# Row E in column tiles of TensorE, and another order of loads at the start of a fused Fourier and gated feed-forward kernel

## The chip, the cores and the metric

The kernel runs on one core of one Trainium2 chip. The metric is the device time of one execution in microseconds (us), as the median of several runs; lower is better. The engines are TensorE (PE, with its weight loads as PEld), VectorE (DVE), ScalarE (ACT), GpSimd (POOL) and SyncE (SP, which here only issues transfers). They run side by side, each through its own instructions in order, and wait for each other by semaphores.

## What is computed

The reference, cut to what matters:

```python
x: (8, 3008, 256) float32
X = fft(fft(x, axis=1), axis=2).real        # (8, 3008, 256)
t = X.reshape(24064, 256)
gate = 1 / (1 + exp(-(t @ w_gate)))         # w_gate, w_val: (256, 1536)
val = t @ w_val
return (gate * val) @ w_out                 # w_out: (1536, 256)
```

The three weight matrices arrive as float64.

## The kernel before

**The sequence transform.** For each of the eight batches the transform along the 3008 points is a matrix product with cosine and sine tables `st`. The symmetries of the transform leave 1505 of the 3008 rows and a quarter of the points: `fold_ops` adds and subtracts the mirrored parts of `x` (tile `x4`), first along the points, then along the features, on VectorE and GpSimd. Six matmuls of 126 x 377 or 126 x 376 (`half`, even and odd points in banks `ev` and `od`) give one half of a result; one ScalarE copy and two VectorE operations (`places`) spread it over the even or odd columns of one of three tiles of 1505 columns each: `pk` (cosine part), `qk` (sine part) and `ek`. The last, `ek`, is the row E: the transform of the single feature in the middle (feature 128), the same in all 128 partitions.

**Where E comes from.** For batch 0, before, `ek` is computed as `pk` is: the weights of the matmul are feature 128 broadcast to 128 columns, so that all partitions come out equal. For batches 1 to 7 the rows are made at once in the loop (`e_load`, `e_fold`, `e_rows`, `e_out`): a matmul with 7 columns of weights, one for each batch, the rows `er` stored to memory (`ed`), and one row spread over 128 partitions by a transfer when its batch begins (`seq_start`).

**The weights.** The feature transform is merged into the weights: `merge` multiplies a piece of `w_gate` or `w_val` (256 columns) with the table `dt` into `G1` and `G2`, four matmuls into a bank `ps`, two ScalarE copies, and two transfers that turn one row of `G2` into columns `ge`. A piece of `w_out` is brought into seven forms `wf` on ScalarE and GpSimd (`forms`). Before either, a piece must become float32: `weight_load` fetches 512 KB as pairs of integers, `weight_parts` is two ScalarE operations, `weight_join` three VectorE operations and one of GpSimd. There are 18 pieces, in the order of `jobs`.

**The loop.** Its unit is a step `i`: one block of 128 hidden features for 256 columns. `front` makes two products `pa` and `pb` on TensorE, and VectorE computes `ae` (two operations, `ek` times the column `ge` plus `pa`) and two tiles `z`; ScalarE applies the sigmoid; `gate` is the product `h` on VectorE in the step after, and sums `sf` on GpSimd; `back`, four steps behind, multiplies with `wf` into the banks `po`. Twelve steps fill one block of output columns, and `finish` stores it. Banks for `pa`, `pb`, `ps`, `ev` and `od` come from one pool of four. Work beside the steps is listed by hand: `at(i, f)` puts `f` into step i, `pre` puts it ahead of the sigmoid.

**Order at the start.** Nothing reorders instructions: what is written first on an engine runs first. Transfers of SyncE and ScalarE use eight semaphores in turn, so that a transfer may have to wait for the eighth before it. Before, two pieces are loaded first, then `x` of batch 0, the cosine table in two halves, four pieces, the sine table whole, and four more pieces. Pieces 0 and 1 are converted and merged; then batch 0 is folded in two halves of the points, with cosine and E sums after each; the sine sums follow; the conversion of pieces 2 to 8 is placed between the evacuations of the sums. The step after which the loop starts holds the merge of piece 2 alone; pieces 9 to 17 are converted in steps 0 to 8, and merges stand in steps 0 to 8.

Of the kernel before, what the change touches and what calls it, by code (L numbers as in the profile page):

```python
# [45 lines left out]
def kernel(  # L46
# [45 lines left out]
    def mm(o, l, r, start, stop):  # L92
        nc.tensor.matmul(o, l, r, start=start, stop=stop, skip_group_check=True)  # L93
# [19 lines left out]
    ge = const.tile([P, 2, NFT], F32, name="ge")  # L113

    x8 = const.tile([NP, B - 1, 4, NQ], F32, name="x8")
    ed = dram.tile([B - 1, NK], F32, name="ed")

    def load_table(t, nq):
        for q in range(0, NQ, nq):
            nc.sync.dma_start(out=st[:, t, q : q + nq], in_=stab[:, t, q : q + nq])  # L120

    jobs = [(w, c - (w == 2)) for c in range(NPR + 1) for w in range(3)
            if (c if w == 2 else c < NPR)]
    RAW, WS = {}, {}
    shared = {}
    KEEP = 10

    def weight_load(j):  # L130


        w, c = jobs[j]
        src = (moe_w_gate, moe_w_val, moe_w_out)[w]
        src = src[2 * c * P : 2 * (c + 1) * P, :] if w == 2 else src[:, c * WC : (c + 1) * WC]
        src = src.rearrange("(c p) f -> p c f", p=P)

        def some(n, pool, tag):

            key = tag, (j - 6) // 3 if tag == "c7" else 0  # L140
            if key not in shared:
                shared[key] = pool.tile([P, n, 2 * WC], F32, name=f"w{tag}", tag=tag)
            return shared[key]

        if j < KEEP:
            pool, tag = ((zp, "z"), (pqp, ("pk", "qk", "ek")[j % 3]), (op, "os"), (sp, "sf"))[
                j // 3 if j < 6 else j // 2 - 1]
            raw = pool.tile([P, 2, WC, 2], I32, name="raw", tag=tag)
            if j < 6:
                pool, tag = ((app, "ae"), (hp, "h"))[j // 3]  # L150
                ws = pool.tile([P, 2, WC], F32, name="ws", tag=tag)
            else:
                ws = some(3, cp, "c7")[:, (j - 6) % 3].rearrange("p (c f) -> p c f", c=2)
        else:
            both = some(12, xp, "x4")
            r, i = (j - KEEP) % 3 * 2, 6 + (j - KEEP) % 6
            raw = both[:, r : r + 2].rearrange("p a n -> p (a n)").bitcast(I32).rearrange(
                "p (c f w) -> p c f w", c=2, w=2)
            ws = both[:, i].rearrange("p (c f) -> p c f", c=2)
        WS[j] = ws  # L160
        if src.dtype == F32:
            nc.sync.dma_start(out=ws, in_=src)
        else:
            RAW[j] = raw
            nc.sync.dma_start(out=raw.rearrange("p c f w -> p c (f w)"), in_=src.bitcast(I32))

    def weight_parts(j):

        if j in RAW:
            raw, ws = RAW[j], WS[j]  # L170
            lo, hi = raw[:, :, :, 0], raw[:, :, :, 1]
            nc.scalar.activation(ws, hi.bitcast(F32), AF.Abs)
            nc.scalar.activation(lo, lo.bitcast(U32), AF.Copy, scale=2.0 ** -29)

    def weight_join(j):
        if j not in RAW:
            return
        raw, ws = RAW.pop(j), WS[j]
        lo, hi = raw[:, :, :, 0], raw[:, :, :, 1]
        wi = ws.bitcast(I32)  # L180
        ts = nc.vector.tensor_scalar
        ts(out=ws, in0=ws, scalar1=2.0 ** -15, scalar2=HUGE, op0=ALU.max, op1=ALU.min)
        ts(out=wi, in0=wi, scalar1=3, scalar2=0x3FFFFFF8, op0=ALU.logical_shift_left,
           op1=ALU.bitwise_and)
        nc.vector.scalar_tensor_tensor(out=wi, in0=hi, scalar=-(2 ** 30), in1=wi,
                                       op0=ALU.bitwise_and, op1=ALU.bitwise_or)
        nc.gpsimd.tensor_tensor(wi, wi, lo, op=ALU.add)
# [36 lines left out]
    def fold_ops(b, nq):  # L224
# [60 lines left out]
    def half(w, d, blk, sn, rows, other=None):  # L285


        c0, n = ((0, NE), (NE, NO))[blk]
        ev, od = [bank(name, other and other[i])[0:rows, 0:n] for i, name in enumerate(("ev", "od"))]

        def sums(*qs):
            for q in sorted(qs, key=lambda q: q % 2):
                mm((ev, od)[q % 2], w(q), st[:, int(sn), q, c0 : c0 + n], q < 2, q >= NQ - 2)

        def then():
            a = evp.tile([P, NE], F32, name="a", tag="a")[0:rows, 0:n]
            nc.scalar.copy(a, ev)
            return lambda: places(a)

        def places(a):  # L300
            nc.vector.tensor_tensor(d[:, blk : blk + 2 * n - 1 : 2], a, od, op=ALU.add)
            lo, hi = (od, a) if sn else (a, od)
            top = M - blk
            nc.vector.tensor_tensor(d[:, top : top - 2 * NO + 1 : -2], lo[:, 0:NO], hi[:, 0:NO],
                                    op=ALU.subtract)
        return sums, then

    def whole(sums, then):
        sums(*range(NQ))
        return then()  # L310

    def seq_start(b):
        PQE[b] = (pqp.tile([P, NK], F32, name="pk", tag="pk"),
                  pqp.tile([P, NK], F32, name="qk", tag="qk"),
                  pqp.tile([P, NK], F32, name="ek", tag="ek"))
        if b:
            nc.sync.dma_start(out=PQE[b][2], in_=ed[b - 1 : b, :].to_broadcast([P, NK]))

    def seq_group(b, blk, what, other=None):
        return half(lambda q: W[b, blk][what][:, q, :], PQE[b][what], blk, what == 1, P, other)  # L320


    ER = []

    def e_load():
        for b in range(1, B):
# [18 lines left out]
    chunks = [(k0, min(CH, NK - k0)) for k0 in range(0, NK, CH)]  # L345
# [147 lines left out]

    def weight_round(*js):
        for j in js:
            weight_parts(j)
            weight_join(j)
# [24 lines left out]

    per = 2 * NPR * len(chunks)
    side = {}
# [111 lines left out]
```

## Time and profile before

| | us |
|---|---|
| time, median of 3 runs | 2027.57 |
| lowest and highest | 2027.19, 2031.57 |
| span of the profiled execution | 2028.5 |

```profile
## 2 busy tenths in 40 slices
PE   5999999999999999999999999999999999999998
PEld 3788789888998889888898888988889888898888
DVE  6899778987899878997889977999879988898887
ACT  3422222222222222222222222222222222222222
POOL 3679555875569755696457955589446875565655
```

Each digit is the busy share of a fortieth of the span (some 51 us) in tenths. Only the first slice shows TensorE half idle: it is the start, with the loads and the first batch's transform. The second holds the early steps, in which the conversion of the weights is done beside the loop. From there on TensorE is full.

### The profile page before, as it was taken

The page shows a single profiled execution, that of the slowest core. Times are in us where ns is not written, and L with a number is a line of the kernel's source. Part 1 is how long each engine was busy: PE and PEld are TensorE (multiplying, and loading weights), DVE is VectorE, ACT ScalarE, POOL GpSimd, SP SyncE. Part 2 cuts the span into 40 slices and gives each one's busy share as a digit, 9 for nine tenths or more (in the row PEclk, how much of TensorE's full clock was granted, in tenths as well). Part 3 has the DMA queues.
Part 4 walks back from the last instruction along what each step waited for, and adds up shares of the span by engine and source line. Part 5 has one row for each costly group of instructions (what it writes and reads, how often), then busy time and mean ns, then how long its engine had stood idle before and what let it go on. Part 6 is the DMA issues. An engine that isn't in the chain of part 4 may idle for free.

```text
span 2028.5 us, 27347 instructions
## 1 busy us (share of the span) xinstructions
PE 1996.6 (98%) x9168; PEld 1743.3 (86%) x9168; DVE 1754.9 (87%) x3221; ACT 498.5 (25%) x875; POOL 1328.4 (65%) x1675
## 2 busy tenths in 40 slices
PE   5999999999999999999999999999999999999998
PEld 3788789888998889888898888988889888898888
DVE  6899778987899878997889977999879988898887
ACT  3422222222222222222222222222222222222222
POOL 3679555875569755696457955589446875565655
PEclk8999999999999999999999999999999999999999
DMA  8240002100021000200010000201002010000001
GB/s 260 84 74 11 27 11 74 33 12 11 11 81 27 11 11 17 76 26 11 16 60 28 27 16 16 73 10 37 11 11 72 16 31 11 11 16 16 11 16 26
DMA packets 136176, 70.98 MB, mean 35 GB/s; under 512 B 127875, under 2 KB 128131, under 8 KB 133642
## 3 DMA queue, kind: packets, MB, share of 16 engines
q1 hardware_dynamic: 134214, 68.69, 12.6%
q8 instruction: 74, 1.21, 0.3%
q10 hardware_dynamic: 1822, 0.54, 0.1%
q14 instruction: 66, 0.54, 0.1%
HBM read 44.50 MB, written 24.68 MB: 34 GB/s over the span
## 4 chain that ended last, share of the span: by engine, by line
PE 85%; DVE 7%; POOL 4%; DMA 2%; issue 1%; ACT 0%; DVEq 0%; SPq 0%; ACTq 0%; POOLq 0%
PE po L93 37%; PE pa L93 21%; PE pb L93 21%; PE ev L93 3%; PE od L93 3%; DVE ae L364 2%; DVE h L379 2%; DVE z L368 1%; DMA ge<-G 1%; DVE z L367 1%; POOL x L239 1%; POOL x L237 1%; DMA st<-in_stab_dram 1%; POOL sf L384 1%; POOL sf L383 1%
## 5 line engine op out<-in xcount | busy, mean ns | idle before, releaser
L575 ACT ACTIVATE z<-z 128x512 f32<-128x512 f32 (+1 forms) x576 | 358.5, 622 | 1319.1 <-DVE z L368 1319.1
L364 DVE SCALAR_TENSOR_TENSOR ae<-ek,ge,pa 128x256 f32<-128x256 f32 (+1 forms) x1152 | 489.7, 466 | 186.1 <-PE pa L93 181.9
L93 PE MATMUL pb<-qk,G 128*128 128x256 f32 (+1 forms) x2304 | 582.2, 375 | 2.5 <-DVE ae L364 2.5
L93 PE MATMUL pa<-pk,G 128*128 128x256 f32 (+1 forms) x2304 | 581.9, 375 | 0.0
L93 PE MATMUL po<-sf,wf 128*128 128x256 f32 (+1 forms) x2304 | 537.3, 376 | 1.0 <-POOL sf L384 0.2
L93 PEld LDWEIGHTS pa<-pk,G 128*128 128x128 f32 x2304 | 438.5, 190 | 55.9 <-issue 1.3
L93 PEld LDWEIGHTS po<-sf,wf 128*128 128x128 f32 x2304 | 437.2, 190 | 54.8 <-POOL sf L385 4.5
L93 PEld LDWEIGHTS pb<-qk,G 128*128 128x128 f32 x2304 | 438.2, 190 | 52.8 <-DVE ae L364 4.1
L383 POOL TENSOR_TENSOR sf<-h 128x256 f32<-128x256 f32 (+1 forms) x288 | 213.4, 741 | 386.9 <-DVE h L379 386.9
L379 DVE TENSOR_TENSOR h<-z 128x512 f32<-128x512 f32 (+1 forms) x576 | 454.7, 789 | 0.0
L367 DVE TENSOR_TENSOR z<-ae,pb 128x512 f32<-128x512 f32 (+1 forms) x576 | 390.1, 677 | 61.4 <-DVE ae L364 1.4
L93 PE MATMUL po<-h,wf 128*128 128x256 f32 (+1 forms) x1728 | 412.7, 375 | 0.0
L368 DVE TENSOR_TENSOR z<-ae,pb 128x512 f32<-128x512 f32 (+1 forms) x576 | 386.4, 671 | 0.0
L93 PEld LDWEIGHTS po<-h,wf 128*128 128x128 f32 x1728 | 329.1, 191 | 36.4
L381 POOL TENSOR_TENSOR sf<-h 128x256 f32<-128x256 f32 (+1 forms) x288 | 219.1, 761 | 210.0 <-DVE h L379 206.2
L384 POOL TENSOR_TENSOR sf<-sf,h 128x256 f32<-128x256 f32 (+1 forms) x288 | 215.4, 748 | 22.6
L385 POOL TENSOR_TENSOR sf<-h,sf 128x256 f32<-128x256 f32 (+1 forms) x288 | 214.0, 743 | 22.6
L466 ACT COPY c<-po 128x512 f32<-128x512 f32 (+1 forms) x141 | 76.7, 580 | 62.0 <-PE po L93 62.0
L93 PE MATMUL ev<-st,x 126*128 126x377 f32 (+3 forms) x216 | 78.0, 495 | 11.7 <-DMA st<-in_stab_dram 11.7
L426 DVE STREAM_TRANSPOSE os<-c 128x256 f32<-128x256 f32 x192 | 83.9, 437 | 0.2
L93 PE MATMUL od<-st,x 126*128 126x377 f32 (+3 forms) x216 | 75.3, 481 | 0.0
L471 POOL TENSOR_TENSOR c<-c 128x512 f32<-128x512 f32 (+1 forms) x47 | 73.5, 1565 | 0.0
(82 smaller groups left out, 711.4 us busy)
## 6 DMA issues: line engine op xcount, KB each, us to landing
x<-in_xf_dram SPq DMA_DIRECT2D x16, 1512.0 KB
out_dram<-os SPq DMA_DIRECT2D x288, 64.0 KB
ek<-ed SPq DMA_DIRECT2D x7, 752.5 KB
out_dram<-os SPq DMA_DIRECT2D x92, 56.0 KB
st<-in_stab_dram SPq DMA_DIRECT2D x2, 1111.9 KB
st<-in_stab_dram SPq DMA_DIRECT2D x1, 2223.7 KB
raw<-in_moe_w_gate_dram SPq DMA_DIRECT2D x4, 512.0 KB
raw<-in_moe_w_val_dram SPq DMA_DIRECT2D x4, 512.0 KB
```

The costliest lines, as they stand in the source:

```text
L93: nc.tensor.matmul(o, l, r, start=start, stop=stop, skip_group_check=True)
L364: nc.vector.scalar_tensor_tensor(out=ae[:, g], in0=ek[:, ks], scalar=ge[:, g, f : f + 1], in1=pa[:, g], op0=ALU.mult, op1=ALU.add)
L367: nc.vector.tensor_tensor(z[:, :, 0], ae, pb, op=ALU.add)
L368: nc.vector.tensor_tensor(z[:, :, 1, ::-1], ae, pb, op=ALU.subtract)
L379: nc.vector.tensor_tensor(h[:, fh], z[:, 0], z[:, 1], op=ALU.mult)
L381: tt(s[:, 2], h[:, 0, 0], h[:, 0, 1], op=ALU.subtract)
L383: tt(s[:, 0], h[:, 0, 1], h[:, 1, 1], op=ALU.add)
L384: tt(s[:, 1], s[:, 0], h[:, 0, 0], op=ALU.subtract)
L385: tt(s[:, 3], h[:, 1, 0], s[:, 1], op=ALU.subtract)
L426: nc.vector.transpose(os_[:, s, 0:nb, h, :], t[:, slot, 0 : nb * TB])
L466: nc.scalar.copy(t[:, 2 * j : 2 * j + 2, 0:n], PO[j][:, :, 0:n])
L575: nc.scalar.activation(z[:, 0], z[:, 0], AF.Sigmoid)
```

## The change

Four things are changed together.

1. **E of batch 0** is computed as one row instead of 128 equal ones: its matmuls have one column of weights, the row is stored to memory and spread by a transfer, as for the other batches (`ed` gets eight rows, `e_spread`).
2. **Column tiles.** Both E computations (`e_sums`) use the array in four column tiles of 32: the four combinations of half and even or odd points go to partitions 0, 32, 64 and 96 of one bank `pe`, and consecutive matmuls address different tiles. One step of the loop (42) has all twelve matmuls of batches 1 to 7, instead of six each in steps 40 and 42.
3. **Order at the start.** Six pieces of gate and value weights are loaded, converted and merged before anything else; then `x` and the two tables, the sine table in halves too; three more pieces after them. The order of `jobs` has the `w_out` pieces later. Pieces 6, 7 and 8 are converted and used before step 0.
4. **Steps.** Pieces 9 to 17 are converted one a step in steps 1 to 9, and each is used in the step after.

The aim is to take TensorE's work on E and on merges out of the time in which TensorE is the bound, and to have the columns `ge` there before they are asked for.

```diff
-    jobs = [(w, c - (w == 2)) for c in range(NPR + 1) for w in range(3)
-            if (c if w == 2 else c < NPR)]
-    KEEP = 10
+    jobs = [(w, c - 2 * (w == 2)) for c in range(NPR + 2) for w in range(3)
+            if (c >= 2 if w == 2 else c < NPR)]
+    KEEP = 9
...
-            W[b, blk] = (v[:, :, 0:HD], r[:, :, 0:HD],
-                         v[:, :, HD : HD + 1].to_broadcast([NP, NQ, P]))
+            W[b, blk] = (v[:, :, 0:HD], r[:, :, 0:HD], v[:, :, HD : HD + 1])
...
-    def e_rows(blk):
-        if not blk:
-            ER.append(cp.tile([B - 1, NK], F32, name="er", tag="c7"))
-        return whole(*half(lambda q: x8[:, :, 1 + 2 * blk, q], ER[0], blk, False, B - 1))
-
-    def e_out():
-        nc.scalar.dma_start(out=ed, in_=ER.pop())
+    def e_sums(col, b, m, other=None):
+        ps = bank("pe", other)
+        tb = lambda blk, par: (2 * blk + par) * TB
+
+        def sums(*qs):
+            for n in range(max(sum(q % 2 == par for q in qs) for par in range(2))):
+                for blk in range(2):
+                    c0, k = ((0, NE), (NE, NO))[blk]
+                    for par in range(2):
+                        for q in [q for q in qs if q % 2 == par][n : n + 1]:
+                            t = tb(blk, par)
+                            mm(ps[t : t + m, 0:k], col(blk, q), st[:, 0, q, c0 : c0 + k],
+                               q < 2, q >= NQ - 2)
+
+        def then():
...
+            nc.scalar.copy(ev, ps[tb(0, 1) : tb(0, 1) + m, 0:NE])
+            nc.scalar.copy(e1[:, 0:NO], ps[tb(1, 0) : tb(1, 0) + m, 0:NO])
+            return lambda: (places(er, 0, True, ev, ps[0:m, 0:NE]),
+                            last(er, ev, e1[:, 0:NO]))
+
+        def last(er, a, ev):
+            nc.scalar.copy(a[:, 0:NO], ps[tb(1, 1) : tb(1, 1) + m, 0:NO])
+            places(er, 1, False, ev, a[:, 0:NO])
+            nc.scalar.dma_start(out=ed[b : b + m], in_=er)
+        return sums, then
...
-    for j in range(2):
+    for j in range(6):
         weight_load(j)
     load_x(0)
-    load_table(0, NQ // 2)
-    for j in range(2, 6):
-        weight_load(j)
-    load_table(1, NQ)
+    for t in range(2):
+        for q in range(0, NQ, NQ // 2):
+            load_table(t, q)
     for j in range(6, KEEP):
         weight_load(j)
...
-    weight_parts(0)
-    weight_parts(1)
-    weight_join(0)
-    weight_join(1)
-    weight_use(0)
-    weight_use(1)
+    for j in range(6):
+        weight_parts(j)
+        weight_join(j)
+        if j:
+            weight_use(j - 1)
+    weight_use(5)
+    halves = range(NQ // 2), range(NQ // 2, NQ)
     seq_start(0)
-    cos = [seq_group(0, blk, what, (2 * blk, 2 * blk + 1) if what else None)
-           for blk in range(2) for what in (0, 2)]
-    for i, f in enumerate(fold_ops(0, NQ // 2)):
+    first_e = e_sums(lambda blk, q: W[0, blk][2][:, q, :], 0, 1, 0)
+    cos = [first_e] + [seq_group(0, blk, 0) for blk in range(2)]
+    for f, qs in zip(fold_ops(0, NQ // 2), halves):
         f()
         for sums, _ in cos:
-            sums(*range(i * NQ // 2, (i + 1) * NQ // 2))
+            sums(*qs)
     sin = [seq_group(0, blk, 1) for blk in range(2)]
-    for sums, _ in sin:
-        sums(*range(NQ))
-    evacuate = [then for _, then in cos + sin]
-    for then, js in zip(evacuate, ((2, 3, 4), (5,), (), (), (6, 7), (8,))):
-        weight_round(*js)
+    for qs in halves:
+        for sums, _ in sin:
+            sums(*qs)
+    for _, then in cos:
         then()()
+    e_spread(0)
     for j in range(KEEP, KEEP + 3):
         weight_load(j)
-    weight_use(2)
+    for j, (_, then) in zip((6, 7), sin):
+        weight_parts(j)
+        weight_join(j)
+        then()()
+    weight_use(6)
+    weight_use(7)
+    weight_parts(8)
+    weight_join(8)
+    weight_use(8)
...
-    for j in range(9, len(jobs)):
-        pre.setdefault(j - 9, []).append(lambda j=j: weight_parts(j))
-        at(j - 9, lambda j=j: weight_join(j))
-        if KEEP <= j < len(jobs) - 3:
-            at(j - 9, lambda j=j: weight_load(j + 3))
-    for j in range(3, len(jobs)):
-        w, c = jobs[j]
-        at(2 * c + (-3, -2, 1)[w], lambda j=j: weight_use(j))
+    for i, j in enumerate(range(KEEP, len(jobs)), 1):
+        pre.setdefault(i, []).append(lambda j=j: weight_parts(j))
+        at(i, lambda j=j: weight_join(j))
+        if j < len(jobs) - 3:
+            at(i, lambda j=j: weight_load(j + 3))
+        at(i + 1, lambda j=j: weight_use(j))
...
-    split(i0 + 28, e_rows, 0)
-    split(i0 + 30, e_rows, 1)
-    at(i0 + 32, e_out)
+    split(i0 + 30, lambda: whole(*e_sums(lambda blk, q: x8[:, :, 1 + 2 * blk, q], 1, B - 1)))
```

More of the change, by code (lines that the diff above doesn't have):

```diff
@@ L115, with load_table @@
     x8 = const.tile([NP, B - 1, 4, NQ], F32, name="x8")
[L116 to L120, printed above, removed]
-    jobs = [(w, c - (w == 2)) for c in range(NPR + 1) for w in range(3)
-            if (c if w == 2 else c < NPR)]
+    ed = dram.tile([B, NK], F32, name="ed")
+    def load_table(t, q):
+        nc.sync.dma_start(out=st[:, t, q : q + NQ // 2], in_=stab[:, t, q : q + NQ // 2])
+    jobs = [(w, c - 2 * (w == 2)) for c in range(NPR + 2) for w in range(3)
+            if (c >= 2 if w == 2 else c < NPR)]
     RAW, WS = {}, {}
-    shared = {}
-    KEEP = 10
+    mega = []
+    KEEP = 9
     def weight_load(j):
@@ L136, in weight_load @@
         src = src.rearrange("(c p) f -> p c f", p=P)
[L138 to L143, printed above, removed]
         if j < KEEP:
-            pool, tag = ((zp, "z"), (pqp, ("pk", "qk", "ek")[j % 3]), (op, "os"), (sp, "sf"))[
-                j // 3 if j < 6 else j // 2 - 1]
+            pool, tag = (pqp, ("pk", "qk", "ek")[j % 3]) if j // 3 == 1 else (zp, "z")
             raw = pool.tile([P, 2, WC, 2], I32, name="raw", tag=tag)
[L149 to L153, printed above, removed]
-        else:
-            both = some(12, xp, "x4")
+            pool, tag = (hp, "h") if j // 3 == 1 else (app, "ae")
+            ws = pool.tile([P, 2, WC], F32, name="ws", tag=tag)
+        else:
+            if not mega:
+                mega.append(xp.tile([P, 12, 2 * WC], F32, name="mega", tag="x4"))
             r, i = (j - KEEP) % 3 * 2, 6 + (j - KEEP) % 6
-            raw = both[:, r : r + 2].rearrange("p a n -> p (a n)").bitcast(I32).rearrange(
+            raw = mega[0][:, r : r + 2].rearrange("p a n -> p (a n)").bitcast(I32).rearrange(
                 "p (c f w) -> p c f w", c=2, w=2)
-            ws = both[:, i].rearrange("p (c f) -> p c f", c=2)
+            ws = mega[0][:, i].rearrange("p (c f) -> p c f", c=2)
         WS[j] = ws
@@ L277, in fold_ops, with half @@
         for blk, (v, r) in enumerate(parts):
-            W[b, blk] = (v[:, :, 0:HD], r[:, :, 0:HD],
-                         v[:, :, HD : HD + 1].to_broadcast([NP, NQ, P]))
+            W[b, blk] = (v[:, :, 0:HD], r[:, :, 0:HD], v[:, :, HD : HD + 1])
         return ops
     PQE = {}
-    def half(w, d, blk, sn, rows, other=None):
+    def half(w, d, blk, sn):
         c0, n = ((0, NE), (NE, NO))[blk]
-        ev, od = [bank(name, other and other[i])[0:rows, 0:n] for i, name in enumerate(("ev", "od"))]
+        ev, od = bank("ev")[:, 0:n], bank("od")[:, 0:n]
         def sums(*qs):
@@ L295, in then, with places @@
         def then():
-            a = evp.tile([P, NE], F32, name="a", tag="a")[0:rows, 0:n]
+            a = evp.tile([P, NE], F32, name="a", tag="a")[:, 0:n]
             nc.scalar.copy(a, ev)
[L298 to L305, printed above, removed]
-        return sums, then
+            return lambda: places(d, blk, sn, a, od)
+        return sums, then
+    def places(d, blk, sn, ev, od):
+        nc.vector.tensor_tensor(d[:, blk : blk + 2 * ev.shape[1] - 1 : 2], ev, od, op=ALU.add)
+        lo, hi = (od, ev) if sn else (ev, od)
+        top = M - blk
+        nc.vector.tensor_tensor(d[:, top : top - 2 * NO + 1 : -2], lo[:, 0:NO], hi[:, 0:NO],
+                                op=ALU.subtract)
     def whole(sums, then):
@@ L316, in seq_start, with seq_group @@
         if b:
[L317 to L323, printed above, removed]
+            e_spread(b)
+    def seq_group(b, blk, what):
+        return half(lambda q: W[b, blk][what][:, q, :], PQE[b][what], blk, what == 1)
     def e_load():
@@ L334, in e_fold, with e_spread @@
         tt(x8[:, :, 3], x8[:, :, 0], x8[:, :, 2], op=ALU.subtract)
-    def e_rows(blk):
-        if not blk:
-            ER.append(cp.tile([B - 1, NK], F32, name="er", tag="c7"))
-        return whole(*half(lambda q: x8[:, :, 1 + 2 * blk, q], ER[0], blk, False, B - 1))
-    def e_out():
-        nc.scalar.dma_start(out=ed, in_=ER.pop())
+    def e_sums(col, b, m, other=None):
[11 more added lines that the diff above has]
+        def then():
+            er = cp.tile([P, NK], F32, name="er", tag="c7")[0:m]
+            ev = evp.tile([P, NE], F32, name="a", tag="a")[0:m]
+            e1 = evp.tile([P, NE], F32, name="a", tag="a")[0:m]
+            nc.scalar.copy(ev, ps[tb(0, 1) : tb(0, 1) + m, 0:NE])
[7 more added lines that the diff above has]
+        return sums, then
+    def e_spread(b):
+        nc.sync.dma_start(
+            out=PQE[b][2], in_=ed[b : b + 1, :].to_broadcast([P, NK]))
     chunks = [(k0, min(CH, NK - k0)) for k0 in range(0, NK, CH)]
@@ L483 @@
     nc.scalar.dma_start(out=dt, in_=dtab.rearrange("(c p) d -> p c d", p=P))
-    for j in range(2):
+    for j in range(6):
         weight_load(j)
     load_x(0)
-    load_table(0, NQ // 2)
-    for j in range(2, 6):
-        weight_load(j)
-    load_table(1, NQ)
+    for t in range(2):
+        for q in range(0, NQ, NQ // 2):
+            load_table(t, q)
     for j in range(6, KEEP):
         weight_load(j)
[L494 to L497, printed above, removed]
-    weight_parts(0)
-    weight_parts(1)
-    weight_join(0)
-    weight_join(1)
-    weight_use(0)
-    weight_use(1)
+    for j in range(6):
[5 more added lines that the diff above has]
+    halves = range(NQ // 2), range(NQ // 2, NQ)
     seq_start(0)
-    cos = [seq_group(0, blk, what, (2 * blk, 2 * blk + 1) if what else None)
-           for blk in range(2) for what in (0, 2)]
-    for i, f in enumerate(fold_ops(0, NQ // 2)):
+    first_e = e_sums(lambda blk, q: W[0, blk][2][:, q, :], 0, 1, 0)
+    cos = [first_e] + [seq_group(0, blk, 0) for blk in range(2)]
+    for f, qs in zip(fold_ops(0, NQ // 2), halves):
         f()
         for sums, _ in cos:
-            sums(*range(i * NQ // 2, (i + 1) * NQ // 2))
+            sums(*qs)
     sin = [seq_group(0, blk, 1) for blk in range(2)]
-    for sums, _ in sin:
-        sums(*range(NQ))
-    evacuate = [then for _, then in cos + sin]
-    for then, js in zip(evacuate, ((2, 3, 4), (5,), (), (), (6, 7), (8,))):
-        weight_round(*js)
+    for qs in halves:
+        for sums, _ in sin:
+            sums(*qs)
+    for _, then in cos:
         then()()
+    e_spread(0)
     for j in range(KEEP, KEEP + 3):
         weight_load(j)
-    weight_use(2)
+    for j, (_, then) in zip((6, 7), sin):
[7 more added lines that the diff above has]
+    weight_use(8)
     per = 2 * NPR * len(chunks)
```

## The prediction

> **What bounds the kernel now.** I read the shares of the page first, then a table of windows, then the chain of waits, then the timeline around each turn.
>
> ```profile
> PE 1996.6 (98%) x9168; PEld 1743.3 (86%) x9168; DVE 1754.9 (87%) x3221; ACT 498.5 (25%) x875; POOL 1328.4 (65%) x1675
> ...
> 43.80:56.00 12.20, 12.16 (x37) 7.99 (x38) 7.83 (x14) 5.45 (x11) 3.94 (x3) 0.86 0.35 124
> 56.00:105.00 49.00, 46.48 (x212) 39.60 (x211) 45.53 (x77) 24.77 (x57) 33.59 (x41) 1.00 0.27 79
> 105.00:200.00 95.00, 95.00 (x442) 83.84 (x441) 91.16 (x159) 25.02 (x46) 81.28 (x103) 1.00 0.27 46
> ```
>
> From 105 us on TensorE is never idle, so there a matmul removed is time saved. The first 105 us are another matter: 56 us pass before the first `ae` of the loop, and from 56 to 105 VectorE has hardly a gap (45.5 of 49).
>
> ```profile
> 29.38 14.32 DMA st<-in_stab_dram
> 43.84 3.73 PE ev L93 x6
> ...
> 72.85 3.69 DMA ge<-G
> 83.71 3.22 DMA ge<-G
> ```
>
> The chain of waits: the start-up ends on the sine table at 43.84, and twice in the early steps on the tiny `ge` transfers.
>
> ```profile
> 9.35 5.76 PE L93 MATMUL ps<-ws,dt 128*128 128x256 f32 x16 [9.35 <-POOL ws L187]
> 12.43 1.82 DVE L229 TENSOR_TENSOR x<-x 126x765 f32<-126x765 f32 x2 [1.67 <-DMA x<-in_xf_dram]
> 13.16 0.37 ACT L203 COPY G<-ps 128x256 f32<-128x256 f32 x1 [4.35 <-PE ps L93]
> 13.57 1.20 ACTq L206 DMA_DIRECT2D ge<-G  x2
> 18.60 0.95 DVE L229 TENSOR_TENSOR x<-x 126x765 f32<-126x765 f32 x1 [4.26 <-DMA x<-in_xf_dram]
> ...
> 55.99 0.87 DVE L364 SCALAR_TENSOR_TENSOR ae<-ek,ge,pa 128x256 f32<-128x256 f32 x2 [1.52 <-PE pa L93]
> ...
> 104.99 0.86 DVE L364 SCALAR_TENSOR_TENSOR ae<-ek,ge,pa 128x256 f32<-128x256 f32 x2
> ...
> 200.63 2.07 PE L93 MATMUL ev<-st,x 126*7 126x377 f32 x6
> 202.54 2.06 PE L93 MATMUL od<-st,x 126*7 126x377 f32 x6
> 204.53 1.13 PE L93 MATMUL pa<-pk,G 128*128 128x256 f32 x4
> ```
>
> The reader should see when `x` lands (12.4 and 18.6), that ScalarE's first copy of a merged piece comes only at 13.16, when step 0 begins (55.99) and step 10 (104.99), and what half of the E rows costs TensorE: 200.63 to 204.53, 3.9 us, twice (7.8 in all).
>
> **What the Trainium skill says.** (1) *TensorEngine Tiling (Array Packing)*, Key Properties: tiles of the array load weights and multiply independently, but changing the mode drains TensorE. No run here shows the parallel part; the E rows of before take 12 passes x 0.314 = 3.77 of their 3.9 us, so changing costs about 0.1. (2) *TensorE: Matmul & The Clock Gate*, Part 3: matmuls start and end strictly in program order; three column tiles gave 2.38 times. The trace shows each float32 matmul as two passes (12 matmuls, 24 records), so I expect the second pass of one tile to hold back the first of the next. (3) The same page, Part 1: after about 3.4 us of idleness the clock is halved until about as much work has passed. The trace agrees: after 2.9 us idle the six sine passes at 43.84 take 3.73 us, later ones 1.9. (4) *SBUF — State Buffer*, two separate sides: VectorE and GpSimd lock a port against each other. The trace agrees: L183 takes 0.43 us, but 0.83 or 1.40 beside GpSimd.
>
> **The change part by part.**
>
> *Six pieces first.* A piece takes 3.7 us from its first ScalarE operation to the end of the GpSimd join (5.57 to 9.29), VectorE being free after 2.3; then a merge of 1.73 (3.5 with the cold clock), and copies of 0.65. ScalarE's order is conversion of j+1, then the copies of j-1; a conversion (1.22) therefore waits behind the merge two before it. Conversions 2 and 3 also wait for two `ge` issues each (1.2): 13.16 + 0.65 + issues = 14.8 for piece 2; its end at 16.0, copies, issues: 17.6 for piece 3. Merge 2 can start at 14.8 + 3.7 = 18.5, cold after 3.4 us idle, and ends at 22.0; copies to 22.7, conversion 4 to 23.9, copies 3 to 24.5, conversion 5 from 24.5. VectorE is through with join 5 at 24.5 + 2.3 = 26.8, GpSimd at 28.2. Only then, in program order, can VectorE fold `x`. Before, it began at 12.43.
>
> *x after six pieces.* Before, 4.4 MB are there at 18.6, 265 GB/s counted from 2 us. Four more pieces (2.1 MB) put the second half of `x` at 26.5: hidden behind the joins. Up to the last sine half the bytes are the 11.1 MB of before, so the tables land by 43.8 too, and nobody will wait for them.
>
> *Folds.* From 26.8: 1.9 for the first half of `x` (12.43 to 14.34), then 6.9 for the first half of the points (18.60 to 25.47), less 0.5 because GpSimd's operation is nearer its end: 35.1. Its share of the second half ends 5.5 later (30.93 against 25.47): 40.6.
>
> *Cosine, E and sine sums.* Pair by pair 24 passes of E for batch 0 become column tiles. With only one pass overlapped by the next tile (factor 2) half of them cost 12 x 0.316/2 + 0.3 = 2.2 us, 3.8 cold. Cosine 12 matmuls at 0.633 = 7.6, sine 7.6. TensorE: 35.1 + 3.8 (E, cold) + 3.8 + 2.2 + 3.8 + 7.6 = 56.3; about 0.3 for changes of mode, and 0.8 because ScalarE copies the cosine banks, which the sine needs, only after the E row's copies, VectorE's four operations and the store's issue. S = 57.4, where before the sums ended at 53.4.
>
> *Pieces 7 and 8 ahead of step 0.* On TensorE both merges stand before the first `pa`, and they are chained. Join 7 stands on VectorE behind the places of the first sine group (end S-0.8): it ends at S+0.8, GpSimd at S+2.1, merge 7 at S+3.9. ScalarE copies it (0.65) before it converts piece 8 (0.66 until VectorE may start); VectorE S+6.9, GpSimd S+8.2, merge 8 from there. TensorE has then stood 4.3 us, so it is cold: S+11.7. `pa` 0.87, and `ae` starts 1.07 after `pa`: T0 = S+12.7 = 70.1 against 55.99. Queued behind merge 8 is the whole loop. The loads for this (piece 8 at 12.6 MB, about 50 us; the row `ek` of 0.75 MB behind it, about 56) are earlier, and so hidden.
>
> *Steps 0 to 9.* Nine pieces are converted in the loop, before and after. Without the waits for `ge` (1.8 us on VectorE) steps 0 to 9 of before take 47.2. After: step 0 has no join (2.2), nine steps with join at the mean of before's (5.04) 45.4, less some 0.4 as GpSimd's forms of piece 6 are gone: 47.2. Five merges fewer in the loop (8.7 us of TensorE) give nothing while VectorE bounds these steps. So step 10 begins at 117.3; TensorE reaches the steady stretch (`pa` of step 12) about 1.4 later instead of 1.9, at 118.7, against 106.86: +11.8.
>
> *E rows in the loop.* 24 passes at 0.314 become 12 x 0.316 + 0.3 + 0.2 = 4.3 instead of 7.8: -3.5. The extra ScalarE copy and the four small VectorE operations lie beside TensorE's steps.
>
> Sum: 2027.6 + 11.8 - 3.5 = 2035.9.
>
> **Rivals.**
> - B, the four tiles overlap fully: E costs 24 x 0.316/4 + 0.4 = 2.3 in the loop (-5.5), and 1.9 less in the start-up: 2027.6 + 9.9 - 5.5 = 2032.0. For it: the order of matmuls, four different tiles in a row; against it: two passes each. With a warm clock in the chain of pieces 7 and 8 it would be 2030.
> - C, no overlap at all: E in the start-up 5.5 cold plus 3.8, instead of 6.0 (+3.3), and nothing in the loop: 2027.6 + 15.1 = 2042.7.
> - D, faster: if TensorE, not VectorE, bounded steps 4 to 8 (with its merge a step has 4.97 us of TensorE against 5.04 of VectorE, so it is near), the merges' 8.7 and the `ge` waits' 1.8 come back; with a tail warm throughout and conversions that don't queue behind merges, T0 is 65 rather than 70: 2027.6 + 9.0 - 8.7 - 1.8 - 3.5 = 2022.6. Against it: VectorE's row is without gaps in the timeline from 56 to 105, but for `ge`.
>
> **How the numbers follow.** A 0.50, B 0.22, C 0.13, D 0.15. The time is A's. The range: S and the clock may each be 2 us off, the joins beside GpSimd 2; the cold merges (1.7 twice) could be warm, the tile overlap 2 or 5.5. 2027 is the warm B with the joins 3 us cheaper, 2043 is C; D and the rest stay outside. Slower than 2031.6: A nearly whole, C, half of B: 0.68; within 0.2%: 0.18; faster: 0.14.
>
> **What would show it.** The first `ae` near 70 instead of 56; VectorE's first fold near 27; two gaps of TensorE between the last sine matmul and the first `pa`, each ended by GpSimd's join; no wait for `ge` in the steps; step 10 some 47 us after step 0; the E matmuls in one stretch of about 4.3 us near step 42. It is wrong if `ae` starts before 60, if steps 0 to 9 shrink well under 45 us, or if the E stretch stays at 7.8.

## The result and the profile after

| | before | after |
|---|---|---|
| time, median of 4 runs each, us | 2027.53 | 2045.70 |
| lowest and highest, us | 2027.19, 2031.57 | 2045.27, 2047.88 |
| span of the profiled execution, us | 2028.5 | 2043.5 |

The ratio after to before is 1.0087, with a 95% interval of 1.0070 to 1.0105: slower by 0.9%. The direction was forecast; the size was not: 2045.7 stands against a forecast of 2035.9 and lies above the upper end of the range, 2043.

The first lines of the page of after are nearly those of before:

```profile
PE 1995.4 (98%) x9168; PEld 1737.3 (85%) x9168; DVE 1756.5 (86%) x3221; ACT 499.8 (24%) x877; POOL 1332.4 (65%) x1675
...
PEclk8799999999999999999999999999999999999999
```

TensorE's busy time went down by 1.2 us while the span grew by 15. So in sum the loss is TensorE standing still, not TensorE working more, and the totals can't say where. The table of windows of after does (stretch, length, then the busy time of PE, PEld, DVE, ACT and POOL, the granted clock, the DMA share, GB/s):

```profile
60.00:75.00 15.00, 10.55 (x37) 8.28 (x36) 4.62 (x10) 3.35 (x7) 2.45 (x4) 0.66 0.23 83
75.00:125.00 50.00, 37.48 (x158) 31.86 (x157) 43.76 (x69) 21.56 (x45) 31.67 (x38) 0.86 0.22 64
125.00:200.00 75.00, 74.57 (x345) 64.93 (x344) 72.44 (x127) 18.70 (x34) 61.70 (x75) 1.00 0.31 50
```

From 125 us all is as before. From 75 to 125, in the early steps, TensorE has 12.5 us of gaps and VectorE 6.2, and the clock is 0.86. Before, the corresponding 49 us showed VectorE busy for 45.5 and the clock at 1.00. When both candidates for the bound have gaps, neither bounds the stretch alone; the chain of waits further down shows what stands between them.

The timeline of after shows the turns that the prediction named (in brackets the idle time before an instruction, and what ended it):

```profile
27.02 2.90 DVE L217 TENSOR_TENSOR x<-x 126x765 f32<-126x765 f32 x2
...
55.80 1.43 PE L93 MATMUL od<-st,x 126*128 126x376 f32 x4
59.53 2.77 PE L93 MATMUL ps<-ws,dt 128*128 128x256 f32 x8 [2.31 <-POOL ws L175]
66.75 3.78 PE L93 MATMUL ps<-ws,dt 128*128 128x256 f32 x8 [4.45 <-POOL ws L175]
70.33 1.28 PE L93 MATMUL pa<-pk,G 128*128 128x256 f32 x4
71.72 0.87 DVE L376 SCALAR_TENSOR_TENSOR ae<-ek,ge,pa 128x256 f32<-128x256 f32 x2 [6.52 <-PE pa L93]
...
87.89 3.67 PE L93 MATMUL ps<-mega,dt 128*128 128x256 f32 x8 [10.24 <-POOL mega L175]
91.40 1.03 PE L93 MATMUL pa<-pk,G 128*128 128x256 f32 x4
92.47 0.87 DVE L376 SCALAR_TENSOR_TENSOR ae<-ek,ge,pa 128x256 f32<-128x256 f32 x2 [2.75 <-PE pa L93]
...
105.07 3.62 PE L93 MATMUL ps<-mega,dt 128*128 128x256 f32 x8 [2.28 <-POOL mega L175]
...
125.98 0.86 DVE L376 SCALAR_TENSOR_TENSOR ae<-ek,ge,pa 128x256 f32<-128x256 f32 x2
227.97 2.09 PE L93 MATMUL pe<-st,x 126*7 126x377 f32 x24
229.98 1.13 PE L93 MATMUL pa<-pk,G 128*128 128x256 f32 x4
```

Each stretch set against before, from `ae` and `pa` starts and the E stretch in the two traces:

| stretch | before, us | after, us | difference | forecast |
|---|---|---|---|---|
| up to the first `ae` | 55.99 | 71.72 | +15.7 | +14.1 |
| first `ae` to `ae` of step 10 | 49.0 | 54.3 | +5.3 | -1.8 |
| from there to the steady stretch (`pa` of step 13) | 4.9 | 4.6 | -0.3 | -0.5 |
| E rows of batches 1 to 7 | 7.8 | 2.0 | -5.8 | -3.5 |
| sum | | | +14.9 | +8.3 |

The sum, 14.9, is the 15.0 by which the spans differ. The medians differ by 18.2: the profiled execution of before was 2.7 us slower than its median, that of after 0.4 us faster, and these 3.2 us stand in no line of the table. The third line runs to step 13, because after still has a gap ahead of `pa` of step 12, to which the prediction reckoned; up to step 12 its difference is -1.0.

The second line carries most of the error. Its excess sits in three steps: 3 (8.7 us from its `ae` to the next), 6 (7.2) and 9 (6.1), where the prediction's mean for a step with a join was 5.04. The first two of these hold the two cold merges at 87.89 and 105.07. The chain of waits of after through step 3 (start, length, what) shows what the first of them waited for:

```profile
81.54 0.85 POOL sf L395
82.40 0.07 issue
82.47 0.81 POOL sf L396
83.27 0.07 issue
83.34 1.05 POOL sf L397
84.39 1.24 POOL wf L201 x3
...
85.71 0.44 POOL wf L201
86.16 1.69 POOL mega L175
87.85 0.04 issue
87.89 3.67 PE ps L93 x8
91.56 0.88 PE pa L93 x4
92.44 0.02 issue
92.47 0.89 DVE ae L376 x2
```

Read it from the end. `ae` waits for `pa`. `pa` stands on TensorE behind the merge of piece 10. The merge waits for GpSimd's share of the join (L175). On GpSimd that share stands behind three sums `sf` and behind four forms `wf` of the output piece 9 (L201), which was converted one step earlier. TensorE has been idle for 10 us by then and works at half the clock (0.51 granted from 87.89 to 91.40): eight passes take 3.67 us where a merge at full clock takes 1.7 to 1.9. Below, a merge at full clock is called warm and one at half clock cold.

### The profile page after: what moved, and what is told of

The parts are those of the page before. It is cut to its first block, busy times and chain, and to the rows that moved or that the text cites. A ratio compares the mean times of both kernels' runs of the same rounds, so it can differ in the third digit from the quotient of the medians.

```text
span 2043.5 us, 27361 instructions
## 1 busy us (share of the span) xinstructions
PE 1995.4 (98%) x9168; PEld 1737.3 (85%) x9168; DVE 1756.5 (86%) x3221; ACT 499.8 (24%) x877; POOL 1332.4 (65%) x1675
## 3 DMA queue, kind: packets, MB, share of 16 engines
q1 hardware_dynamic: 134498, 69.46, 12.5%
## 4 chain that ended last, share of the span: by engine, by line
PE 84%; DVE 9%; POOL 5%; issue 1%; ACT 0%; DMA 0%; DVEq 0%; ACTq 0%; POOLq 0%
PE po L93 36%; PE pa L93 21%; PE pb L93 20%; PE ev L93 3%; PE od L93 3%; DVE ae L376 2%; DVE h L391 2%; DVE z L380 2%; PE ps L93 1%; DVE z L379 1%; POOL x L227 1%; POOL x L225 1%; POOL sf L396 1%; POOL sf L395 1%; DVE os L438 0%
## 5 line engine op out<-in xcount | busy, mean ns | idle before, releaser
L93 PE MATMUL ev<-st,x 126*128 126x377 f32 (+1 forms) x192 | 67.9, 486 | 0.8 <-ACT a L284 0.8
L93 PE MATMUL od<-st,x 126*128 126x377 f32 (+1 forms) x192 | 66.6, 479 | 0.0
```

## The experiments

Theory 1, formed from this trace: the loss beyond the forecast comes from using a piece one step after its conversion. Its rivals: the loss in the steps is a matter of cold clock or of transfers that later use would not mend, or of VectorE having more to do. The other runs take apart the start (tail, order of conversion), E's column tiles, and what is left when the costs are taken out. Each ratio is to the kernel before on the same chip.

**use_later**: every piece that is converted in steps 1 to 9 is used two steps after its conversion.

```diff
-        at(i + 1, lambda j=j: weight_use(j))
+        at(i + 2, lambda j=j: weight_use(j))
```

> The changed kernel with each piece of steps 1 to 9 used two steps after its conversion instead of one; nothing else. Theory 1 (a merge right after its conversion makes TensorE wait for GpSimd's join, and start cold): TensorE's waits for GpSimd ahead of the merges of pieces 10 and 13 go (10.2 and 2.3 us), step 10 begins some 47 to 49 us after step 0 instead of 54.3, time 2038 to 2041. Theory 2 (the steps are long because VectorE and GpSimd hinder each other in nine steps with a conversion): the stretch stays within 1 us of 54.3 and the time at 2045 to 2046.

Measured: 2044.44, ratio 1.0075 (1.0058 to 1.0092). Step 10 comes 48.0 us after step 0, within theory 1's 47 to 49. Yet the whole gains only 0.12% of the time, the two kernels' intervals overlap, and the median lies above theory 1's 2038 to 2041. The timeline of use_later shows both the cure and the new illness:

```profile
82.30 1.99 PE L93 MATMUL ps<-mega,dt 128*128 128x256 f32 x8 [0.71 <-POOL mega L175]
...
104.60 1.99 PE L93 MATMUL ps<-mega,dt 128*128 128x256 f32 x8 [0.84 <-POOL mega L175]
...
114.78 1.97 PE L93 MATMUL po<-h,wf 128*128 128x256 f32 x4 [2.94 <-ACT wf L202]
117.69 1.22 PE L93 MATMUL po<-h,wf 128*128 128x256 f32 x2 [0.93 <-POOL wf L201]
```

The waits of 10.24 and 2.28 are down to 0.71 and 0.84 and those merges are nearly warm. But the forms of an output piece are now made so late that `back` in step 10 waits for them, and `pa` of step 11 stands behind it: `pa` of step 13 comes 58.4 us after the first `ae`, against 58.9 in after. So the waits ahead of the merges are cured, and a remedy must spare the output pieces; whether the cause is right, the next run has to show.

**gates_later**: only gate and value pieces used two steps later, forms still one step later.

```diff
-        at(i + 1, lambda j=j: weight_use(j))
+        at(i + (1 if jobs[j][0] == 2 else 2), lambda j=j: weight_use(j))
```

> The changed kernel with the gate and value pieces of the steps merged two steps after their conversion, the output pieces formed one step after, as in the change. The run with all pieces two steps later lost its gain to a wait for the forms in step 11. Theory 1 (the merges' waits for the join are the 7 us by which steps 0 to 9 are too long): step 10 begins 47 to 49 us after step 0, no wait for wf of more than 1 us, and step 13's first product comes 5 to 7 us nearer to the first ae than in the changed kernel (58.9 us after it); time 2038 to 2041. Rival (GpSimd's backlog turns up elsewhere): under 2 us gained.

Measured: 2040.78, ratio 1.0058 (1.0040 to 1.0076). From the first `ae` to `pa` of step 13 it takes 53.9 us instead of 58.9: -5.0, as theory 1 wants. Step 10 comes after 49.2, just beyond the forecast of 47 to 49, because one merge still waits and is cold, as the timeline of gates_later shows:

```profile
88.19 3.68 PE L93 MATMUL ps<-mega,dt 128*128 128x256 f32 x8 [2.83 <-POOL mega L175]
```

So 5.0 of the 7.1 us by which the steps missed the forecast are the distance between join and merge. The time, 2040.78, is inside the expected 2038 to 2041.

**tail_open**: piece 8 is converted before the uses, and pieces 7 and 8 are merged in steps 0 and 1 instead of ahead of step 0.

```diff
-    weight_use(6)
-    weight_use(7)
     weight_parts(8)
     weight_join(8)
-    weight_use(8)
+    weight_use(6)
...
+    at(0, lambda: weight_use(7))
+    at(1, lambda: weight_use(8))
```

> The changed kernel with piece 8 converted before the merges of pieces 7 and 8, and these merges moved behind the first products of steps 0 and 1. Theory 1 (the chain merge 7, copies, conversion 8, join 8, merge 8 ahead of the first product costs some 10 us): the first ae at 60 to 63 us instead of 71.7, time 2034 to 2037. Rival (VectorE and GpSimd bound the early steps, and what the start gains is lost there, since the two merges and forms then stand beside the conversions): first ae early too, but the time falls by under 5 us, to 2041 or more.

Measured: 2035.45, ratio 1.0030 (1.0019 to 1.0041). The timeline of tail_open at the turn:

```profile
55.88 1.43 PE L93 MATMUL od<-st,x 126*128 126x376 f32 x4
57.15 1.03 PE L93 MATMUL pa<-pk,G 128*128 128x256 f32 x4
...
59.62 1.99 PE L93 MATMUL ps<-ws,dt 128*128 128x256 f32 x8
...
61.72 0.87 DVE L376 SCALAR_TENSOR_TENSOR ae<-ek,ge,pa 128x256 f32<-128x256 f32 x2 [0.68 <-PE ps L93]
```

`pa` follows the last sine matmul at once, and a merge behind it is warm (1.99 instead of 2.77 and 3.78). The first `ae` comes at 61.72, 10.0 us earlier than in after; the steps stay about as long as they were (54.9 up to step 10, 54.3 in after). The chain of pieces 7 and 8 therefore costs about 10 us by itself, of which the steps give 0.6 back.

**conv_first**: the six pieces are all converted before any of them is merged.

```diff
         weight_join(j)
-        if j:
-            weight_use(j - 1)
-    weight_use(5)
+    for j in range(6):
+        weight_use(j)
```

> The changed kernel with all six conversions at the start placed ahead of all six merges. Theory 1 (conversions queue behind the merges' copies on ScalarE, and hold back the folds): VectorE's first fold at 19 to 21 us instead of 27.0, the first half of the folds then waits for the second half of x and ends at 33 to 34 instead of 36.8, the first ae 2 to 4 us earlier, time 2041 to 2044. Rival (loads of x or tables are as late, or the cosine sums wait for the GpSimd share of the folds anyway): first ae within 1 us of 71.7, time 2045 to 2046.

Measured: 2039.08, ratio 1.0049 (1.0034 to 1.0064). VectorE's timeline in conv_first:

```profile
19.95 0.69 DVE L173 SCALAR_TENSOR_TENSOR ws<-raw,ws 128x512 int32<-128x512 int32 x1
20.56 2.90 DVE L217 TENSOR_TENSOR x<-x 126x765 f32<-126x765 f32 x2
...
25.07 0.94 DVE L217 TENSOR_TENSOR x<-x 126x765 f32<-126x765 f32 x1
```

The first fold starts at 20.56 instead of 27.02. The expectation let the second half of `x` hold the folds back; in fact the operation on that half follows at 25.07 without a wait, so the first `ae` comes 6.2 us earlier (65.57), more than the 2 to 4 expected, and the time too is below the expected 2041 to 2044. ScalarE's copies between conversions, which wait for merges, thus cost some 6 us of the start.

**all_fixed**: the three edits tail_open, conv_first and gates_later together in after.

> The changed kernel with all three: conversions first, the merges of pieces 7 and 8 behind the first products, gate and value pieces merged two steps later. If the three costs are separate and add up: 3 + 10 + 6 us less than the changed kernel, 2025 to 2028. If VectorE's and GpSimd's work is the common bound behind them: 2030 or more.

Measured: 2023.99, ratio 0.9972 (0.9962 to 0.9983), now faster than before and somewhat below the expected 2025 to 2028. In the profiles the three costs apart are 10.0, 6.2 and 5.0, 21.2 us in sum; together they took 21.7 off the median (2045.70 to 2023.99). By the ratios, each taken on one chip, the three edits gain 0.57, 0.38 and 0.29% (some 11.6, 7.7 and 5.9 us, each known to about 5), and all together 1.15% (23.3 us). Within that they add up. The windows of all_fixed:

```profile
60.00:75.00 15.00, 9.86 (x34) 7.09 (x33) 14.48 (x24) 6.40 (x14) 10.26 (x12) 0.81 0.25 70
75.00:125.00 50.00, 48.53 (x220) 41.64 (x219) 48.34 (x81) 19.94 (x43) 37.34 (x48) 0.99 0.37 105
```

VectorE is full again in both stretches, as it was before the change, and the clock is back at 0.99 in the second. What is left of the change, some 5.6 us (0.28%), is about what the E rows save in the loop. So even the mended start gains nothing of note: its first `ae` comes at 54.29 (55.99 in before), and step 10 comes 49.7 us later (49.0).

**tiles_alone**: before, with only the E rows of the loop put into the four column tiles. The twelve matmuls are those of after; `e_sums` replaces `e_rows` and `e_out` as in the change.

```diff
...
-    split(i0 + 28, e_rows, 0)
-    split(i0 + 30, e_rows, 1)
-    at(i0 + 32, e_out)
+    split(i0 + 30, lambda: whole(*e_sums(lambda blk, q: x8[:, :, 1 + 2 * blk, q], B - 1)))
```

> The kernel before, with only the E rows of batches 1 to 7 in four column tiles in one step; start, loads and steps as before. Theory 1 (the stretch of E is on TensorE's path and shrinks from 7.8 to 2.0 us): time 2021 to 2023. Rival (the third ScalarE copy between VectorE's operations and the one bank make the products after it wait, and eat part of it): 2024 to 2027.

**tile_major** and **tile_pairs**: after, with another order of the same matmuls. In tile_major all three of one tile come before the next tile's; in tile_pairs two tiles alternate, then the other two.

```diff
-            for n in range(max(sum(q % 2 == par for q in qs) for par in range(2))):
-                for blk in range(2):
-                    c0, k = ((0, NE), (NE, NO))[blk]
-                    for par in range(2):
-                        for q in [q for q in qs if q % 2 == par][n : n + 1]:
+            for blk in range(2):
+                c0, k = ((0, NE), (NE, NO))[blk]
+                for par in range(2):
+                    if True:
+                        for q in [q for q in qs if q % 2 == par]:
```

```diff
-            for n in range(max(sum(q % 2 == par for q in qs) for par in range(2))):
-                for blk in range(2):
+            for blk in range(2):
+                for n in range(max(sum(q % 2 == par for q in qs) for par in range(2))):
```

> The changed kernel with the same E matmuls in the same column tiles, but all of one tile before the next. Theory 1 (tiles overlap because consecutive matmuls address different tiles, and starts keep the program's order): the E stretch of the loop grows from 2.0 to 7 or 8 us, the start by 2 to 5, time 2052 to 2056. Rival (the array runs ahead to any tile that is free, whatever the order): the stretch stays near 2 us and the time at 2045 to 2046.

> The changed kernel with the E matmuls ordered in pairs of tiles: tiles 0 and 1 in turn, then 2 and 3. Theory (a tile's matmuls wait in the array without holding back other tiles, up to three passes of one tile; from the starts seen with one tile after the other): tiles 2 and 3 start with the third pass of 0 and 1, the stretch is 8 x 0.316 = 2.5 us. Rival (the program's order of starts is kept): two tiles at a time, 12 x 0.316 = 3.8 us.

The E stretch in the timelines of tiles_alone, tile_major and tile_pairs, one after the other, each with the matmul that follows:

```profile
208.82 2.09 PE L93 MATMUL pe<-st,x 126*7 126x377 f32 x24
210.84 1.13 PE L93 MATMUL pa<-pk,G 128*128 128x256 f32 x4
```

```profile
229.71 4.01 PE L93 MATMUL pe<-st,x 126*7 126x377 f32 x24
233.65 1.13 PE L93 MATMUL pa<-pk,G 128*128 128x256 f32 x4
```

```profile
223.27 2.73 PE L93 MATMUL pe<-st,x 126*7 126x377 f32 x24
225.93 1.13 PE L93 MATMUL pa<-pk,G 128*128 128x256 f32 x4
```

From start to start the stretch is 2.02, 3.94 and 2.66 us, for the same 24 passes. tiles_alone gives 2024.89, ratio 0.9974 (0.9964 to 0.9983): with the ratio's interval 3 to 7 us less than before, and 5.8 less in the stretch. By its time alone it falls among the rival's 2024 to 2027, but on this chip before stood at 2028.84, and theory 1's 2021 to 2023 fits a before of some 2027.5; of the rival's wait the trace shows nothing, as `pa` follows the stretch at once. tile_major's stretch fell between its two expectations: the order matters, but even the worst of the three orders takes half the time of before. (Its time, 2045.66, ratio 1.0077, is the rival's, but its single times, 2042.04 to 2048.79, are too far apart to tell 2 us.) Its single passes show why; which tile a pass belongs to is read from the order and the even spacing of the starts. The first tile's six follow each other at 0.32 us. The second tile's first pass starts at 230.361, with the first tile's third (230.355), the third tile's at 231.008, the fourth's at 231.656: about 0.65 us, two passes, after one another. When a later tile starts, three passes of the tile before it, earlier in the program, are still waiting. From this I took that up to three waiting passes of one tile do not hold back a later tile, and expected 2.5 us for tile_pairs; it took 2.66 (one run, 2041.09 us), and there tiles 3 and 4 start with the third passes of 1 and 2. When the order alternates between all four tiles, as in the change, four passes start within 0.02 us of each other, and the next four 0.32 us later.

**sine_halves, tiles_ge, tiles_halves_ge**: what else of the change's aims helps before? The sine table and sums in halves are a part of the change. That `ge` is there before it is asked for is had here in another way, by issuing its transfers ahead of the next load of weights. All three kernels start from before.

```diff
-    load_table(1, NQ)
+    load_table(1, NQ // 2)
...
-    for sums, _ in sin:
-        sums(*range(NQ))
+    for h in range(2):
+        for sums, _ in sin:
+            sums(*range(h * NQ // 2, (h + 1) * NQ // 2))
```

```diff
-        if KEEP <= j < len(jobs) - 3:
-            at(j - 9, lambda j=j: weight_load(j + 3))
...
         at(2 * c + (-3, -2, 1)[w], lambda j=j: weight_use(j))
+    for j in range(KEEP, len(jobs) - 3):
+        at(j - 9, lambda j=j: weight_load(j + 3))
```

> The kernel before with three things: the E rows of the loop in four column tiles, the sine table and sums in halves, and in the steps the ge transfers issued ahead of the next weight load. Theory (the tile gain of 5.8 stays, the sine sums end 4 to 5 us earlier but VectorE's conversions let only 1 to 3 of these through, the ge waits of 1.8 us go): 2017 to 2022. Rival (the start is bound by VectorE and the loads alone): the same as with the tiles alone, 2023 to 2026.

> The kernel before with the sine table and the sine sums in two halves, nothing else. If it is this that brought the first ae from 56 to 50.7 us in the run with three changes: first ae at 50 to 53 us, time 3 to 6 us under before. If that was the ge order or the tiles: first ae at 55 to 57, and the time within 1.5 us of before.

> The kernel before with the E rows in column tiles and the ge transfers ahead of the next load, the sine table whole. Since the sine halves alone changed nothing: the gain over the tiles alone is that of the ge waits, 1 to 2 us, 2021 to 2024, and level with the next run within 2 us. If the halves help once TensorE is not cold at step 0: 3 us or more over the next run.

> The three-part version of before once more (tiles, sine halves, ge ahead of loads), on the same chip as the run without the halves. If its 2019.1 was the start's luck: 2021 to 2024, first ae back at 54 or later. If not: 2017 to 2021.

| kernel | median, us | ratio | interval |
|---|---|---|---|
| tiles_halves_ge (tiles, halves, `ge` order) | 2019.12 | 0.9954 | 0.9936 to 0.9971 |
| best_again (the same kernel) | 2022.58 | 0.9961 | 0.9949 to 0.9974 |
| tiles_ge (tiles, `ge` order) | 2021.98 | 0.9958 | 0.9944 to 0.9971 |
| sine_halves (halves alone) | 2029.76 | 1.0003 | 0.9995 to 1.0012 |

The halves alone give nothing: the first `ae` comes earlier (54.11), but step 0 then takes 5.1 us instead of 3.7, so step 1 starts at 59.24 against 59.69. In that step 0 `pb` waits 2.35 us for VectorE's `qk`, and TensorE is then at half the clock for 3.41 us. With tiles and the `ge` order, the halves add nothing either: the second measurement of the full version is level with tiles_ge, and the 2019.12 of the first is not to be relied on. In the profile of best_again step 0 has the same wait (2.36 us) and the same halved clock, in that of tiles_halves_ge neither, with the same instructions. The `ge` order shows in the steps: 47.6 us from step 0 to step 10 in tiles_ge against 49.0 before. The version to keep is before with the column tiles and this order alone, at 0.42% under before (about 8 us), with nothing of the change's start in it. Its interval overlaps those of tiles_alone and of all_fixed, so its lead over them isn't shown.

## Why the prediction was right or wrong

- **Six pieces and the folds**: right. VectorE's first fold starts at 27.02 (forecast 26.8), because ScalarE's conversions stand behind copies that wait for merges; conv_first, which takes just this away, starts it at 20.56.
- **x hidden, tables waited for by nobody**: right in after. The estimate of 26.5 us for the second half of `x` was too late, as conv_first folds it at 25.07 with no wait. It changed nothing in the forecast of after, but it is why I expected too little of conv_first.
- **End of the sums**: the last sine matmul ends at 57.2 (forecast 57.4). That this is so near is partly luck: the second half of the E passes took 1.4 us instead of 2.2, and the first cosine half, partly at half the clock, 4.9 instead of 3.8.
- **Pieces 7 and 8**: right in mechanism and nearly in size. Both gaps of TensorE ended by GpSimd's join are there, and the second merge is cold (3.78). The Trainium skill (*TensorE: Matmul & The Clock Gate*, Part 1) gives about 3.4 us of idleness before the clock falls; here 4.45 us gave a fully cold merge, but 2.31 us already gave one of 2.77, between warm and cold. The 2.9 us before the sine sums of before, which the prediction took as agreement, were also less than 3.4. I had priced that first merge as warm, which is 1.0 of the 1.6 us by which the first `ae` came later than 70.1.
- **Waits for `ge`**: gone in after, as forecast.
- **Steps 0 to 9**: this step failed. "Five merges fewer in the loop (8.7 us of TensorE) give nothing while VectorE bounds these steps" took their length from VectorE's work alone, 47.2 us; they took 54.3. Of the rearranged uses I asked what a join costs VectorE and not who waits for its last part: TensorE, which holds `pa` of the next step behind the merge. The join's last part stands on GpSimd behind sums and forms. gates_later took back 5.0 of the 7.1 us with nothing changed but the step of the merges; one late, cold merge of some 2.8 + 1.8 us remains in it. The third long step (9) holds no merge. In its trace VectorE has no wait, but one operation of the conversion (L170) takes 1.51 us instead of 0.42 while GpSimd's join (L175) runs from 122.30 to 124.04; that is about the 1.0 us by which the step is too long. In use_later, where the same operation takes 0.42, step 9 took 4.8 us; no run changes this alone.
- **E rows**: the mechanism was right, the size was off. The factor of overlap was taken as 2, because the Trainium skill (*TensorE: Matmul & The Clock Gate*, Part 3) has matmuls starting and ending strictly in program order. The 24 passes took 2.0 us, a factor of 3.9, and saved 5.8 instead of 3.5 us: rival B's case for this term. Between column tiles the trace contradicts the strict order: in tile_major a later tile's first pass starts with the first tile's third of six, ahead of three passes that are earlier in the program.
- **Rivals and range**: C (no overlap) is refuted by the E stretch, though its time was the nearest. D (faster) rested on TensorE's merges coming back as time saved, and they didn't. No case had the steps longer than before, so the range ended too low. The sum of the table alone, 2027.6 + 14.9 = 2042.5, would have lain just inside the range; the 3.2 us between profiles and medians put the time above it.

In sum the misses are +1.6 (first `ae`), +7.1 (steps), +0.2 (on to the steady stretch) and -2.3 (E): 6.6 us more than the forecast difference of 8.3. The other 3.2 us of the miss in the medians (18.2 against 8.3) lie between profiles and medians. The prediction took its distances from a profile whose execution lasted 2030.25 us and added them to the median of 2027.6; how much of the 2.7 us between these lies in the start is not known.

## What to carry to other kernels

When a piece of work is prepared on one chain of engines and consumed on an engine that runs in order, the price of preparing it late is not its own duration but everything queued behind the waiting consumer; look at the last engine of the chain and at what stands ahead of it there. Give such a piece more than one step, but check the deadline of each consumer: here two steps cured the merges and made the output forms late. And when a change bundles parts, measure them apart: here the column tiles and an earlier `ge` were worth 0.4%, and the new order at the start cost more than that.

## What the hardware showed that I had not expected

- Float32 matmuls in four column tiles overlap wholly if consecutive ones address different tiles: 24 passes of up to 377 columns in 2.02 us, against 7.8 us without column tiles. The order sets the gain: 2.66 us when tiles alternate in pairs, 3.94 tile by tile.
- A wait of 2.3 us can already cost clock, and its length alone does not say how much. Merges of the same eight passes took 1.7 to 1.9 us warm, 2.77 after a wait of 2.31 in after, 3.62 after one of 2.28 at 105.07, and 3.67 after 10.24. In each of the fourteen traces the granted clock changes only at points that lie multiples of 3.41 us apart. In after it fell to half at 60.60, 1.1 us into the merge of 2.77 us, and at 104.98, just ahead of the merge of 3.62 us; in the 3.41 us before these points TensorE had been busy for 1.09 and 1.22 us. Over all traces it fell from full to half after every such stretch with less than 1.4 us of matmuls, and after none with more than 1.54.
- The start is not the same in each execution: with the same instructions up to there, the last sine matmul ended between 54.9 us (use_later) and 57.5 us (gates_later), and the first `ae` came between 68.34 and 71.99. In before, tiles_alone and tiles_ge, whose start is the same, the first `ae` came between 54.42 and 57.60. Differences of up to 3.7 us in the first `ae` between single profiles say nothing by themselves; those of tail_open (10.0) and conv_first (6.2) are larger, and the medians bear them out.
